# Ranks, places and scatters of a routing kernel moved by a step, and GpSimd's weight remainders cut in four

## The chip, the cores and the metric

One core of one Trainium2 chip runs the whole program. The metric is device time of one execution in microseconds, taken from several executions; the kernel before has a median of 978.65 us.

## What is computed

Three layers run one after the other on 2304 tokens (4 sequences of 576) of 512 features. The part that the change touches is the first and the routing of the second:

```
scores = scale * q @ k^T ; bias, causal mask, window of 128     (8 heads of 64)
x      = softmax(scores) @ v                                    -> 2304 x 512
logits = x @ w_gate + log1p(exp(x @ w_noise)) * noise           (8 experts)
top2   = the two largest logits of a token, softmax weights over the two
out    = sum over the two of weight * relu(x @ w1[e]) @ w2[e]   (w1 512x1024, w2 1024x512)
y      = relu(out @ w_in)^2 @ w_out                             (2048 wide, float32 in and out)
```

## The kernel before

**Stages.** For the first 140 us or so the kernel does attention and routing; then the eight experts (until some 600 us), then the last layer. The matmuls of the later stages are float32 products made of three passes: each weight is split into a rounded high part and a remainder. While attention runs, GpSimd splits the first eight weight chunks (`prep_one("pool", "pool")`, lines 97 to 112): a copy of 128x1024 into the rounded type (L108) and a subtraction of 128x1024 for the remainder (L110), two inputs from SBUF.

**The attention loop** (lines 553 to 575) has 36 working steps `v`, each for 128 query rows and 4 of the 8 heads, two steps to a block of 128 tokens. The order is written out by hand; each engine takes its instructions in that order. In step `v` come: `s_step(v+2)`, the score matmuls (L257, on some steps masked columns first, L246) into a double bank of tag "b", and on VectorE four reductions (L262: bias, and the row's extreme) that read this bank, then four exponentials on ScalarE (L268); `t_step(v+1)`, six transposes (L279) into two banks of tag "a" and their copies on ScalarE (L281); the slot 4 of the step; `pv_step(v)`, the products with v (L303) into another "b" bank; `norm` (L314, L317, L320, VectorE), which reads that bank, and every second step a store to DRAM (L326) and loads on SP's queue; `prep_one` on every fourth step; the slot 5. Tag "b" has two banks, so the scores of step `v+1` can start only when the four reductions of step `v` have read theirs. Tag "a" has three banks, tag "c" one.

**Routing** is hung into these steps by `at(step, slot, function, ...)`; slots 0 to 3 lie behind the four reductions of the step on VectorE. A pair `p` is 256 tokens, four steps. With v = 4p+3: the transposes of the block for the gate (`gate_t`, L333, bank "c") stand in slot 4 of steps 4p+3 and 4p+4, the gate's matmuls (`gate_w`, `gate_m`, L344 and L352) in 4p+5, and the selection of two experts (`gate_o`, L363 to L377, VectorE) in slots 0 to 2 of step 4p+6. Of these L363, L375 and L377 read two operands from SBUF. `rank` (lines 379 to 390: ten small matmuls, L387, into bank "c", and two additions to `acc` on VectorE, L390) stands in slot 5 of step 4p+6; `place` (lines 392 to 423: `n` = 0, L397, reads the rank's bank; the rest ends in `pos`, L422) in slots 0 to 3 of step 4p+7. The `scatter` of the pair's first block, two indirect DMAs of GpSimd (L428), stands in slot 3 of step 4p+7, that of the second in step 4p+8.

**The first expert's input.** Rows of the first three tiles are gathered before all tokens are placed: `early_table` reads the slot table back (L501, SP), `gather` fetches the rows (L441, GpSimd), `x_in` transposes them (L448, a bank "a"), copies (L449, ScalarE) and subtracts (L450, VectorE, which is the last reader of that bank). For the first two tiles they stand in steps 17, 18, 20 and 25, 26, 28.

The planner of a step, in lines 521 to 532:

```
        o = v + 2 if end else v + 3
        for n, c in enumerate((0, 0, 0, 1, 2)):
            at(o, c, gate_o, p, n)
        at(o, 4 if end else 5, rank, p)
        for n, c in enumerate((0, 1, 1, 2, 2, 3)):
            at(o + 1, c, place, p, n)
        at(o + 1, 3, scatter, 2 * p)
```

Of the kernel before, what the change touches and what calls it, by code (L numbers as in the profile page):

```python
# [11 lines left out]
F32 = mybir.dt.float32  # L12
# [5 lines left out]
OP = mybir.AluOpType  # L18
# [11 lines left out]
PARTS = (6, 10, 14)  # L30
# [19 lines left out]
def attn_moe_ffn(ctx: ExitStack, tc: tile.TileContext, qt, kt, vt, wgn, noise, w1, w2, w_in, w_out,  # L50
                 consts, out):
    nc = tc.nc
# [18 lines left out]
    def bank(tag):  # L71
        if tag == "b":
            return psum.tile([128, 2, 512], F32, name="psb", tag="b", bufs=2)
        return psum.tile([128, 512], F32, name="ps" + tag, tag=tag, bufs={"a": 3, "c": 1}[tag])
# [13 lines left out]
    def load_to(n):  # L88
        while nload[0] < min(n, len(srcs)):
            i = nload[0]  # L90
            src, a = srcs[i]
            r = rawp.tile([128, 1024], F32, name="raw", tag="raw", bufs=2)
            nc.sync.dma_start(out=r if a is None else r.rearrange("p (a d) -> p a d", a=a), in_=src)
            raws[i] = r
            nload[0] += 1

    def prep_one(hi="act", lo="dve"):
        i = nprep[0]
        nprep[0] += 1
        load_to(i + 1)  # L100
        r = raws.pop(i)
        g, m = (i // 4) % 3, (i % 4) * 2048
        t = big["wb" if g else "wa"] if g < 2 else late["wc"]
        c = [t[:, m:m + 1024], big["wt"] if g == 1 and m == 6144 else t[:, m + 1024:m + 2048]]
        if hi == "act":
            nc.scalar.activation(out=c[0], in_=r, func=AF.Copy)  # L106
        else:
            nc.gpsimd.tensor_copy(c[0], r)  # L108
        eng = nc.vector if lo == "dve" else nc.gpsimd
        eng.tensor_tensor(out=c[1], in0=r, in1=c[0].bitcast(F32), op=OP.subtract)  # L110
        chunks[i] = c
        load_to(i + 2)

# [108 lines left out]
    todo = {}  # L222

    def at(v, slot, f, *a):
        todo.setdefault((v, slot), []).append((f, a))
# [152 lines left out]

    def rank(p):
        oh = G["oh", p]  # L380
        rk = bank("c")[:, 0:16].rearrange("p (q w) -> p q w", q=2)
        G["rk", p] = rk
        for q in range(2):
            terms = [(tri, oh[:, q])] + [(ones, oh[:, 0])] * q + [(ones, acc)]
            for m, (l, r) in enumerate(terms):
                for k in range(2):
                    nc.tensor.matmul(rk[:, q, :], l, r[:, k, :], start=(m + k == 0),  # L387
                                     stop=(m + k == len(terms)))
        for q in range(2):
            nc.vector.tensor_tensor(out=acc, in0=acc, in1=oh[:, q], op=OP.add)  # L390
# [123 lines left out]
    last = NV - 1  # L514
    for p in range(NT // 2):
        v = 4 * p + 3
        end = v == last
        at(v - end, 4, gate_t, 2 * p)
        at(v + 1, 4, gate_t, 2 * p + 1)
        at(v + 2, 0 if end else 4, gate_w, p)  # L520
        at(v + 2, 0 if end else 5, gate_m, p)
        o = v + 2 if end else v + 3
        for n, c in enumerate((0, 0, 0, 1, 2)):
            at(o, c, gate_o, p, n)
        at(o, 4 if end else 5, rank, p)
        for n, c in enumerate((0, 1, 1, 2, 2, 3)):
            at(o + 1, c, place, p, n)
        at(o + 1, 3, scatter, 2 * p)
        if end or 2 * p + 2 == PARTS[-1]:
            at(o + 1, 4, scatter, 2 * p + 1)  # L530
        else:
            at(o + 2, 3, scatter, 2 * p + 1)
    at(3, 3, more_consts)
    at(4, 4, zero_rows)
    for j, (v, w, x) in enumerate(((17, 18, 20), (25, 26, 28), (2 * PARTS[-1] + 3, 2 * PARTS[-1] + 4, last + 1))):
        at(v, 4, early_table, j)
        at(w, 5, gather, 0, j, True)
        at(x, 5, x_in, 0, j)
# [14 lines left out]
    for v in range(-2, NV + 3):  # L553
        s_step(v + 2, v)
        if 0 <= v + 1 < NV:
            t_step(v + 1)
        run(v, 4)
        if 0 <= v < NV:
            i, g = divmod(v, 2)
            pv_step(v)  # L560
            for n in range(3):
                norm(i, g, n)
            if g:
                if nq < NT:
                    load_q(nq)
                    nq += 1
                while nv < 5 * B and v_free(nv - 5) <= 2 * i + 1:
                    load_v(nv)
                    nv += 1
                if nk < B and 2 * i + 1 >= 9 * (nk - 1) + 1:  # L570
                    load_k(nk)
                    nk += 1
            if v % 4 == 2 and nprep[0] < 8:
                prep_one("pool", "pool")
        run(v, 5)
# [33 lines left out]
    for c in range(16):  # L609
        c = 8 * (c % 2) + c // 2  # L610
# [85 lines left out]
    def side_work(e, f):  # L696
        if f % 2 == 1 and nprep[0] < 8 * e + 12 and (e, f) != (E - 1, 7):
            prep_one()
        if e:
            next(decode, None)  # L700
        if e and e + 1 < E and f >= 3:
            gather(e + 1, f - 3)
# [251 lines left out]
    last = E - 1  # L954
    for e in range(last):
        if e == 0:
            py = bank("c")
            for f in range(8):
                mm2(0, 0, f, py)
                if f in (4, 5):  # L960
                    x_in(0, f - 1)
                if f in (5, 7):
                    prep_one()
            y_out(0, 0, py)
            for j in range(NJ):
                gather(1, j)
# [163 lines left out]
    end = 56 * NSB  # L1130
# [85 lines left out]
    for n, (s, u, kk) in enumerate(batches):  # L1216
# [8 lines left out]
        for k in range(2):  # L1225
            st, en = kk + k == 0, kk == 3 and k == 1
            for m, (p, o, lead) in enumerate(((P1, b13[:, 0:256], True), (P2, b26[:, 0:256], True),
# [8 lines left out]
                late_ = (3 * s + u) % 2  # L1236
                if m == 0:
                    p1, u3 = tmp[2 + late_][:, 0:256], tmp[late_][:, 0:256]
                    x, y = [rows.tile([128, DM], F32, name="x", tag="r", bufs=6) for _ in range(2)]
# [71 lines left out]
```

## Time and profile before

| | |
|---|---|
| median of 3 executions | 978.65 us (977.57 to 979.04) |
| the profiled execution | 978.19 us, span 976.1 us |
| TensorE matmul busy | 957.3 us (98%) |
| VectorE busy | 674.8 us (69%) |
| ScalarE busy | 463.8 us (48%) |
| GpSimd busy | 419.2 us (43%) |

The span is what the profiler sees of the program; some 2 us of the execution lie around it. Busy time of TensorE includes the modelled ends of pipelined matmuls, so a wait shorter than such an end doesn't show as idle time; the starts of the instructions show it. In the timeline a row gives the start, the length, the engine, the line, the operation, the operands and, in brackets, the idle time before it and what ended it.

### The profile page before, as it was taken

The numbers are of one execution on the slowest core, as the hardware profiler recorded it, in microseconds if no ns is written. First come the engines' busy times: TensorE is split into PE (matmuls) and PEld (weight loads), VectorE is DVE, ScalarE is ACT, GpSimd is POOL, SyncE is SP. The second block draws the span as 40 slices with busy tenths as digits, with TensorE's granted clock in tenths as the row PEclk, the third lists the DMA queues.
The fourth block names the chain that finished last, engine by engine and source line by source line (L and its number), as shares of the span: only waits on it lengthen the run. The fifth ranks groups of instructions, "written<-read, shape, count | busy, mean of one in ns | idle before, by whom it ended". The sixth has DMA issues, their size and how long they took to land. (4 is left out here: it accounts for less than half of the span.)

```text
span 976.1 us, 19647 instructions
## 1 busy us (share of the span) xinstructions
PE 957.3 (98%) x7438; PEld 879.1 (90%) x7438; DVE 674.8 (69%) x1432; ACT 463.8 (48%) x887; POOL 419.2 (43%) x453
## 2 busy tenths in 40 slices
PE   8899999999999999999999999999999999999998
PEld 6677779898998989899898898999999998999998
DVE  5777754757686776766764436778576999877773
ACT  6677743434343343433343446655554564434331
POOL 0665543124242333425334032624221667988880
PEclk9999999999999999999999999999999999999999
DMA  8777525456667575656555453976538774444331
GB/s 277 273 237 279 198 88 152 135 166 226 197 212 241 161 234 197 219 204 207 202 190 200 148 174 94 299 203 181 151 99 240 227 213 156 145 140 129 130 108 44
DMA packets 118198, 179.99 MB, mean 184 GB/s; under 512 B 11232, under 2 KB 66288, under 8 KB 117712
## 3 DMA queue, kind: packets, MB, share of 16 engines
q1 hardware_dynamic: 107120, 146.77, 46.9%
q0 software_dynamic: 10976, 31.90, 10.6%
q8 instruction: 59, 0.97, 0.4%
q14 instruction: 43, 0.35, 0.1%
HBM read 124.33 MB, written 54.30 MB: 183 GB/s over the span
## 5 line engine op out<-in xcount | busy, mean ns | idle before, releaser
L872 POOL TENSOR_TENSOR gs<-xb 128x256 f32<-128x256 f32 x72 | 69.5, 985 | 29.3 <-DVE wc L872 13.0
L476 ACT ACTIVATE ha<-psa 128x384 fp32r<-128x384 f32 x64 | 31.3, 491 | 93.3 <-PE psa L472 91.8
L268 ACT ACTIVATE p<-p,mx 128x192 f32<-128x192 f32 x144 | 57.6, 450 | 30.3 <-DVE mx L262 29.5
L689 POOL TENSOR_TENSOR et<-ex,et 128x512 f32<-128x512 f32 x16 | 20.9, 1304 | 112.3 <-DVE ex L685 112.3
L710 POOL DMA_INDIRECT yr<-yg,pos x36 | 36.1, 1003 | 68.4 <-DVE ha L477 44.9
L477 DVE SCALAR_TENSOR_TENSOR ha<-psa,ha 128x384 fp32r<-128x384 f32 x64 | 35.4, 553 | 43.0 <-ACT ha L476 38.0
L428 POOL DMA_INDIRECT slots<-tok,pos x36 | 35.0, 972 | 46.1 <-DVE rs L314 29.6
L472 PE MATMUL psa<-xa,wa 128*128 128x384 f32 x288 | 53.4, 336 | 0.3 <-DVE ha L477 0.3
L472 PE MATMUL psa<-xa,wc 128*128 128x384 f32 x288 | 53.4, 336 | 0.0
L791 PE MATMUL psb<-wa,ha 128*128 128x512 f32 x216 | 52.8, 396 | 0.0
L441 POOL DMA_INDIRECT xr<-xd,gidx x40 | 44.3, 1108 | 19.2 <-issue 6.0
L262 DVE CUSTOM_DVE_ANT_0 p<-psb,bias 128x192 f32<-128x192 f32 x144 | 45.8, 352 | 7.7 <-PE psb L257 6.8
L472 PEld LDWEIGHTS psa<-xa,wa 128*128 128x128 f32 x288 | 49.4, 188 | 0.6 <-DVE ha L477 0.5
L472 PEld LDWEIGHTS psa<-xa,wc 128*128 128x128 f32 x288 | 49.6, 188 | 0.2
L795 ACT ACTIVATE yo<-psb 128x512 f32<-128x512 f32 x38 | 22.7, 598 | 54.3 <-PE psb L791 40.8
L872 DVE TENSOR_TENSOR wc<-gs,wc 128x512 fp32r<-128x512 f32 x48 | 48.5, 1049 | 0.0
L689 POOL TENSOR_TENSOR ex<-ex 128x512 f32<-128x512 f32 x12 | 15.6, 1303 | 74.8 <-DVE ex L685 74.8
L886 POOL DMA_DIRECT2D raw<-w x49 | 27.2, 560 | 47.0 <-DVE wb L872 18.4
L791 PEld LDWEIGHTS psb<-wa,ha 128*128 128x128 f32 x216 | 39.5, 188 | 7.8
L791 PE MATMUL psb<-wb,ha 128*128 128x512 f32 x176 | 46.3, 398 | 0.0
L110 DVE TENSOR_TENSOR wa<-raw,wa 128x1024 fp32r<-128x1024 f32 x20 | 25.3, 1266 | 30.0 <-ACT wa L106 29.9
L303 PEld LDWEIGHTS psb<-v,pt 64*64 64x64 f32 (+1 forms) x1056 | 33.1, 136 | 11.6 <-issue 7.9
(327 smaller groups left out, 2742.6 us busy)
## 6 DMA issues: line engine op xcount, KB each, us to landing
raw<-in_w_dram SPq DMA_DIRECT2D x64, 512.0 KB, 5.3
xb<-gmid SPq DMA_DIRECT2D x72, 256.0 KB, 2.7
v<-in_vt_dram SPq DMA_DIRECT2D x20, 520.0 KB, 6.7
yg<-yo SPq DMA_DIRECT2D x40, 256.0 KB, 2.5
raw<-w POOLq DMA_DIRECT2D x36, 256.0 KB, 3.9
gmid<-yo SPq DMA_DIRECT2D x48, 192.0 KB
ex<-in_w_in_dram SPq DMA_DIRECT2D x16, 512.0 KB, 4.4
ex<-in_w_out_dram SPq DMA_DIRECT2D x16, 512.0 KB, 3.4
```

Of the source, the lines that this page charges most:

```text
L262: nc.vector.tensor_tensor_reduce(out=p2[j][:, a, :], in0=ps[:, a, j, :], in1=bias[:, 4 * g + 2 * j + a, :], op0=OP.add, op1=OP.min, scale= ...
L268: nc.scalar.activation(out=p2[j][:, a, :], in_=p2[j][:, a, :], func=AF.Exp, bias=mx[j][:, a:a + 1], scale=-1.0)
L303: nc.tensor.matmul(px[64 * x:64 * x + 64, a, j, :], l, r, start=not any(m[:2] == (x, a) for m in mms[:n]), stop=not any(m[:3] == (x, a, j) ...
L428: st = nc.gpsimd.indirect_dma_start(out=slots, out_offset=bass.IndirectOffsetOnAxis(ap=pos[:, i, k:k + 1], axis=0), in_=tok[:, i:i + 1], i ...
L441: nc.gpsimd.indirect_dma_start(out=XR[e, j], out_offset=None, in_=xd[0:PARTS[j] * 128] if early else xd, in_offset=bass.IndirectOffsetOnAx ...
L472: nc.tensor.matmul(o, w[wp][:, f * 128:(f + 1) * 128], x[:, xp, d, :], start=(n == 0), stop=(n == 11))
L476: nc.scalar.activation(out=hi, in_=ps, func=AF.Relu)
L477: nc.vector.scalar_tensor_tensor(out=lo, in0=ps, scalar=0.0, in1=hi.bitcast(F32), op0=OP.max, op1=OP.subtract)
L689: nc.gpsimd.tensor_tensor(out=x, in0=af, in1=cf, op=OP.add)
L710: nc.gpsimd.indirect_dma_start(out=YR[i, k], out_offset=None, in_=yg, in_offset=bass.IndirectOffsetOnAxis(ap=pos[:, i, k:k + 1], axis=0))
L791: nc.tensor.matmul(py, h[:, hq], wc[wp][:, wsl], start=(f + n == 0), stop=(f == 7 and n == 2))
L872: f(**a)
```

## The change

`rank` of the pairs 0 to 5 goes from slot 5 of step 4p+6 to slot 4 of step 4p+7, ahead of what stands there, and uses a bank of tag "a" (for all pairs). For these pairs `place` 0 goes to slot 5 of step 4p+7 and the other places to slots 0 to 2 of step 4p+8; the scatters go to steps 4p+8 and 4p+9. The pairs 6 to 8 keep their order. For the first two tiles the table, the gather and `x_in` stand in steps 18, 19, 22 and 26, 27, 30. GpSimd subtracts a weight remainder in four pieces of 128x256.

```diff
@@ -106,8 +106,10 @@
-        eng = nc.vector if lo == "dve" else nc.gpsimd
-        eng.tensor_tensor(out=c[1], in0=r, in1=c[0].bitcast(F32), op=OP.subtract)
+        eng, step = (nc.vector, 1024) if lo == "dve" else (nc.gpsimd, 256)
+        for n in range(0, 1024, step):
+            sl = slice(n, n + step)
+            eng.tensor_tensor(out=c[1][:, sl], in0=r[:, sl], in1=c[0][:, sl].bitcast(F32), op=OP.subtract)
@@ -378,7 +380,7 @@
-        rk = bank("c")[:, 0:16].rearrange("p (q w) -> p q w", q=2)
+        rk = bank("a")[:, 0:16].rearrange("p (q w) -> p q w", q=2)
@@ -522,17 +524,24 @@
-        at(o, 4 if end else 5, rank, p)
-        for n, c in enumerate((0, 1, 1, 2, 2, 3)):
-            at(o + 1, c, place, p, n)
-        at(o + 1, 3, scatter, 2 * p)
+        late_ = 2 * p + 2 < PARTS[-1]
+        q = o + 2 if late_ else o + 1
+        if late_:
+            todo.setdefault((o + 1, 4), []).insert(0, (rank, (p,)))
+            at(o + 1, 5, place, p, 0)
+        else:
+            at(o, 4 if end else 5, rank, p)
+            at(q, 0, place, p, 0)
+        for n, c in enumerate((0, 1, 1, 2, 2) if late_ else (1, 1, 2, 2, 3)):
+            at(q, c, place, p, n + 1)
+        at(q, 3, scatter, 2 * p)
         if end or 2 * p + 2 == PARTS[-1]:
-            at(o + 1, 4, scatter, 2 * p + 1)
+            at(q, 4, scatter, 2 * p + 1)
         else:
-            at(o + 2, 3, scatter, 2 * p + 1)
+            at(q + 1, 3, scatter, 2 * p + 1)
-    for j, (v, w, x) in enumerate(((17, 18, 20), (25, 26, 28), (2 * PARTS[-1] + 3, 2 * PARTS[-1] + 4, last + 1))):
+    for j, (v, w, x) in enumerate(((18, 19, 22), (26, 27, 30), (2 * PARTS[-1] + 3, 2 * PARTS[-1] + 4, last + 1))):
```

## Rows read from the trace of the kernel before

**Rows 1.** Busy time by stretch: time, length, PE, PEld, DVE, ACT, POOL, PEclk, DMA, GB/s.

```profile
50.00:100.00 50.00, 48.45 (x885) 36.69 (x882) 37.53 (x236) 39.92 (x104) 29.62 (x40) 1.00 0.74 253
...
150.00:200.00 50.00, 50.00 (x294) 44.40 (x293) 26.24 (x44) 19.05 (x30) 10.60 (x10) 1.00 0.53 164
```

**Rows 2.** Waits of PE, whole span: us in total, times, longest.

```profile
PE psc L387 <- DVE oh L375: 1.7, 5, 0.6
```

**Rows 3.** Timeline of step 14 (pair 2, the step 4p+6), PE and DVE.

```profile
58.33 0.88 PE L257 MATMUL psb<-k,q 64*64 64x192 f32 x16
...
59.39 0.36 DVE L262 CUSTOM_DVE_ANT_0 p<-psb,bias 128x192 f32<-128x192 f32 x1 [0.61 <-PE psb L257]
...
59.95 1.13 PE L303 MATMUL psb<-v,pt 128*64 128x65 f32 x32
...
61.14 0.18 DVE L375 TENSOR_TENSOR oh<-iota,sel 128x32 bf16<-128x32 uint32 x1
61.25 0.15 DVE L377 TENSOR_TENSOR gap<-gs 128x2 f32<-128x2 f32 x1
...
61.39 0.20 PE L387 MATMUL psc<-oh,tri 128*128 128x8 bf16 x2 [0.31 <-DVE oh L375]
...
61.59 0.08 DVE L262 DVE_READ_ACCUMULATOR2_ANT mx<- 128x1 f32 x1
...
61.82 0.88 PE L257 MATMUL psb<-k,q 64*64 64x192 f32 x16
```

**Rows 4.** Timeline of step 15 (pair 2, the step 4p+7), PE, DVE and POOL.

```profile
62.76 0.36 DVE L262 CUSTOM_DVE_ANT_0 p<-psb,bias 128x192 f32<-128x192 f32 x1
...
63.92 1.13 PE L303 MATMUL psb<-v,pt 128*64 128x65 f32 x32
...
64.94 0.08 DVE L262 DVE_READ_ACCUMULATOR2_ANT mx<- 128x1 f32 x1
64.94 0.16 DVE L422 TENSOR_TENSOR pos<-gs,cst 128x4 int32<-128x4 f32 x1
...
65.07 0.30 PE L246 MATMUL psb<-far,ones 64*64 64x256 bf16 x4
...
65.37 0.99 POOL L428 DMA_INDIRECT slots<-tok,pos  x1 [5.44 <-DVE rs L314]
```

**Rows 5.** Timeline of step 6 (pair 0, the step 4p+6), DVE and PE.

```profile
30.94 2.31 DVE L377 TENSOR_TENSOR gap<-gs 128x2 f32<-128x2 f32 x1
...
33.58 0.30 PE L246 MATMUL psb<-far,ones 64*64 64x256 bf16 x2 [2.09 <-DVE mx L262]
```

**Rows 6.** Busy time and clock in step 7, columns as in rows 1.

```profile
34.50:37.00 2.50, 2.50 (x14) 2.15 (x14) 2.27 (x18) 1.58 (x5) 0.00 (x0) 0.50 0.92 371
```

**Rows 7.** Timeline around step 18 (pair 3): GpSimd's chunk and VectorE's L363.

```profile
70.19 1.06 POOL L108 CAST wb<-raw 128x1024 fp32r<-128x1024 f32 x1
...
71.33 2.35 POOL L110 TENSOR_TENSOR wb<-raw,wb 128x1024 fp32r<-128x1024 f32 x1
...
73.26 0.45 DVE L363 TENSOR_TENSOR gs<-gs,nz_sb 128x16 f32<-128x16 f32 x1
```

**Rows 8.** GpSimd's subtractions of line 653: ns minimum/median/maximum, first and last start.

```profile
L653 POOL TENSOR_TENSOR tt<-et,tt x16: 722/741/815, 372.9 to 526.9; 128x256 f32<-128x256 f32 x16
```

**Rows 9.** Timeline, end of step 12 and start of step 13, PE.

```profile
53.64 1.13 PE L303 MATMUL psb<-v,pt 128*64 128x65 f32 x32
...
54.59 0.83 PE L257 MATMUL psb<-k,q 64*64 64x192 f32 x16
```

**Rows 10.** Timeline: `x_in` behind step 20; copies of the transposes of step 30.

```profile
82.24 0.66 PE L448 MATMUL psa<-cst,xr 128*128 128x128 f32 x4
...
83.67 0.69 DVE L450 TENSOR_TENSOR xa<-psa,xa 128x512 fp32r<-128x512 f32 x1 [0.46 <-ACT xa L449]
...
118.12 0.85 ACT L281 ACTIVATE pt<-psa 128x384 f32<-128x384 f32 x2
```

**Rows 11.** Waits of SP's queue, 0 to 160 us: us in total, times, longest.

```profile
SPq L501 <- DMA slots<-tok,pos: 19.4, 3, 11.5
```

## The prediction

> **What bounds the kernel now.** I read the busy time by stretch first. In the experts' stretch TensorE is busy all of the time, in attention 48.45 of 50 us, at the full clock [rows 1]. So what attention gains or loses in TensorE's order of work reaches the end: behind it no idle time stands that could take it up or give it back. The waits of TensorE come next: the rank's matmuls wait for VectorE's one-hot five times, 1.7 us in all [rows 2]. This is the wait that the new order removes, and the most that this list promises.
>
> Then I read the timeline of one pair, since a busy share doesn't tell which wait ends last. In step 14 (4p+6) the scores start at 58.33, the first reduction at 59.39, L375 at 61.14, L377 at 61.25, the rank's matmuls at 61.39; the last reduction's readout ends at 61.59 + 0.08 = 61.67 and the next scores start at 61.82 [rows 3]. So when the rank has run, the bank of the scores has just come free: both wait for the same VectorE work. The six pairs from 1 to 6 all show the next scores within 0.15 us of the last readout. In step 15 (4p+7), with `place` between the reductions, the readout ends at 64.94 + 0.08 = 65.02 and the next scores start at 65.07 [rows 4]: VectorE again, by a little. A pair has one or two steps bound by the chain scores, reductions, bank, scores; the others are TensorE's.
>
> **The parts.** The profiled execution took 978.19 us, 0.46 under the median of the three; the sum is made against it.
>
> (a) Four pieces, pair 0. L377, 0.15 us elsewhere [rows 3], takes 2.31 us in step 6, and the next scores follow it after a wait of 2.09 [rows 5]. It reads two operands from SBUF; GpSimd began a subtraction just ahead of it, and L377 ends with it. [...] The same is seen smaller at pair 3: L363 starts inside a subtraction of 2.35 us that begins at 71.33 and, at 73.26 + 0.45 = 73.71, ends 0.03 behind it [rows 7]. A piece of 128x256 takes 0.74 us [rows 8], so L377 waits for at most one: 2.31 - 0.74 = 1.57, of which I take 1.5. With some 1.2 us of idle time left instead of 2.1 and more, I take the clock to stay up: 1.2 more. Sum -2.7 (bounds 0, were a second piece and the slow clock to follow, and -3.4, were L377 to wait for none). For GpSimd itself 4 x 0.74 - 2.35 = 0.6 us more a chunk, eight times; nothing waits for the chunks before the experts, so I cost this at nothing. Without that cover it would be 4.9.
>
> (b) Rank out of step 4p+6. The next scores still wait for the last readout. By step 15 they can follow it by 0.05 instead of 0.15 [rows 3, 4]: six times 0.07, -0.4 (bounds 0, and the -1.7 of the wait list).
>
> (c) Rank into step 4p+7. `place` is gone from the reductions there, so TensorE's own work sets the step. Scores can follow the products by 0.95 (53.64 to 54.59) [rows 9], here they take 65.07 - 63.92 = 1.15 [rows 4], so 0.20 is free. The rank takes 61.82 - 61.39 = 0.43 of TensorE's order [rows 3], some 0.3 of it issue. So +0.1 a pair, +0.6 (bounds -1.2 and +2.6). The two additions to `acc` move with it, behind the reductions, where VectorE has time.
>
> (d) `place` into step 4p+8. The chain from the first reduction to the last readout stays, 65.02 - 62.76 = 2.26 [rows 4]: of its small operations L397 leaves it and L422 comes in. But `norm` and L397 now stand ahead of the first reduction of a step that follows a full TensorE step, so I put this reduction 1.1 behind the scores, not the 0.94 of step 15 (62.76 - 61.82) [rows 3, 4]. With 0.1 to the next scores that is 3.5 us, against 3.25 for the place step before (65.07 - 61.82) and about that for the 4p+8 steps: +0.2 for five pairs, and some 0.6 for pair 0, whose step 8 is short of work: +1.6 (bounds 0 and +3). The scatters go with it, behind each other on GpSimd in the same order. SP waits for their landing ahead of the table read, 19.4 us in three waits [rows 11]; read and scatter move together, and the stores and loads behind the read have a step's time, so I cost this at nothing. Without that cover a late load of q would stop TensorE for a microsecond or so.
>
> (e) `x_in` two steps later. Its transposes leave steps 20 and 28, 0.66 us each [rows 10], some 0.6 of it issue; I take -1.25 for both. They go to steps 22 and 30, whose TensorE idles for the chain, so their own time is free. Their banks are not. The last reader is L450 on VectorE, 0.69 us, behind a copy on ScalarE [rows 10], which stands behind the copies of the transposes; those run late in a 4p+6 step, from 118.12 for 0.85 us in step 30 [rows 10], when the next scores have started. Behind step 22 the rank of pair 4 needs that very "a" bank, three allocations on, and would wait about 1.0. In step 30 the rank of pair 6 stands ahead of `x_in` and takes a bank, so the transposes wait for the first copy of 118.12 and push the first reduction of the following place step by 1.8. Sum -1.25 + 1.0 + 1.8 = +1.55 (bounds -1.25 and +3).
>
> (f) The collision. GpSimd's chunk follows the four scatters of a pair without a pause: L422 at 64.94 [rows 4], copy at 70.19, subtraction at 71.33 [rows 7], 6.39 behind L422. L422 moves into the next step and one reduction forward, to 2.9 behind its scores. So the pieces run from 2.9 + 6.4 = 9.3 to 12.3 behind the scores of step 4p+8. The selection of the next pair is two steps on, 3.5 + 3.7 = 7.2 (the second from 54.59 to 58.33 [rows 9, 3]), with L375 2.81 and L377 2.92 behind its scores [rows 3]: 10.0 and 10.1. Before, the subtraction ended just ahead of or within L363; now L375 and L377 fall into its pieces. The first goes at the end of the running piece, almost at once; the second then faces a whole one, 0.74 [rows 8]. The last reduction stands behind L377, and the next scores behind that: six pairs (1 to 6) times 0.74 = +4.4 (bounds 0, and two waits and a blocked L363, 1.6 a pair, +9.6). I take one piece, as both instructions are nearest to the case of L377 in rows 5. In exchange the tails of the long subtraction on L363 go (0.45 at pair 3 instead of 0.17, smaller twice): -0.5.
>
> Sum: -2.7 - 0.4 + 0.6 + 1.6 + 1.55 + 4.4 - 0.5 = +4.55. Against the profiled execution that is 982.7, against the median 983.2: **983.0 us**.
>
> **Rivals.** *The copy blocks too.* L363 stands 1.34 behind its scores, 8.5 on the scale of (f), inside GpSimd's copy (8.2 to 9.3). No row of before shows an instruction with two SBUF inputs beside a copy. Were it held as by a subtraction, L363 would wait 0.75 and L375 and L377 0.85 more: (f) is 6 x 1.6 = 9.6, the time 978.2 + 0.15 + 9.6 = 988.0. [...]
>
> [...]
>
> [...]
>
> *The clock falls each time.* The steps 4p+6 then idle TensorE by 0.6 + 0.74 and more; were 1.25 lost behind each as in rows 6, 983.0 + 7.5 = 990.5. Against it: it was seen only behind 2.1.
>
> **How the numbers follow.** Forecast 0.50, copy 0.13, miss 0.20, miss with free banks 0.12, clock 0.05. The range from 976.5 to 988.0 holds the first three with the bounds of the small terms (about 1.8 below the miss, and the copy's sum above) and leaves out the last two, 0.17. A measurement of this kernel can tell 0.2%, 1.96 us. Faster: the 0.12 and 0.04 of the miss, 0.16; same: 0.14 of the miss and 0.03 of the forecast, 0.17; slower: 0.67.
>
> **What would show it.** Right: L377 of step 6 near 0.8 instead of 2.31 and no clock of 0.50 behind it; the scores behind steps 10, 14, ... still within 0.1 of the last readout; L375 or L377 of these steps at 0.5 us and more beside GpSimd's pieces; the rank of pair 4 waiting for L450. Wrong: L375 and L377 at their 0.15 to 0.2 in most pairs, steps 4p+6 shorter than 3.3, or a 4p+7 step that grows by the whole rank.

## The result, and the profile after

The changed kernel takes **993.22 us** (median of 6 runs, 986.88 to 995.26) against 978.71 for the kernel before in the same session (6 runs): a ratio of 1.014, 95% interval 1.0118 to 1.0163. It is slower, as forecast, but by 14.5 us where the forecast of 983.0 had some 4, and outside the range of 976.5 to 988.0. Its profiled execution took 989.1 us (span 987.0, mean granted clock 0.995).

Busy time by stretch, columns as in rows 1:

```profile
50.00:100.00 50.00, 42.90 (x770) 33.38 (x768) 37.06 (x220) 34.52 (x88) 25.09 (x40) 0.97 0.66 221
100.00:150.00 50.00, 43.57 (x698) 34.14 (x699) 33.42 (x194) 30.04 (x77) 26.47 (x44) 0.93 0.42 130
```

In attention TensorE was busy 48.45 of 50 us [rows 1]; now it is 42.90, and its granted clock is no longer full (PEclk 0.97 and 0.93). The waits of PE over the whole span (us in total, times, longest) say for whom:

```profile
PE psb L259 <- DVE rs L316: 7.9, 7, 1.9
PE psb L248 <- DVE mx L264: 4.3, 5, 1.7
PE psa L450 <- ACT pt L283: 1.4, 1, 1.4
...
PE psa L389 <- DVE oh L377: 0.7, 1, 0.7
PE psa L389 <- DVE xa L452: 0.7, 1, 0.7
```

The rank's wait of rows 2 has fallen from 1.7 to 0.7, with another 0.7 for a bank of `x_in`. In its place the scores (L248, L259: L246 and L257 of before) wait for VectorE twelve times, 1.0 us on average; before, the list had one such wait, the 2.09 of rows 5. Three instructions of VectorE make it late. By line: ns minimum/median/maximum, first and last start (L365, L377 and L379 are L363, L375 and L377 of before):

```profile
L365 DVE TENSOR_TENSOR gs<-gs,nz_sb x9: 174/599/748, 27.7 to 147.5; 128x16 f32<-128x16 f32 x9
...
L377 DVE TENSOR_TENSOR oh<-iota,sel x9: 191/294/307, 29.3 to 148.6; 128x32 bf16<-128x32 uint32 x9
...
L379 DVE TENSOR_TENSOR gap<-gs x9: 155/728/732, 29.5 to 148.7; 128x2 f32<-128x2 f32 x9
```

The timeline of step 14 (the step of rows 3) shows how:

```profile
57.14 1.05 POOL L108 CAST wa<-raw 128x1024 fp32r<-128x1024 f32 x1
...
57.66 0.58 DVE L365 TENSOR_TENSOR gs<-gs,nz_sb 128x16 f32<-128x16 f32 x1
...
58.28 2.77 POOL L112 TENSOR_TENSOR wa<-raw,wa 128x256 fp32r<-128x256 f32 x4
...
59.44 0.29 DVE L377 TENSOR_TENSOR oh<-iota,sel 128x32 bf16<-128x32 uint32 x1
...
59.66 0.73 DVE L379 TENSOR_TENSOR gap<-gs 128x2 f32<-128x2 f32 x1
...
60.59 0.08 DVE L264 DVE_READ_ACCUMULATOR2_ANT mx<- 128x1 f32 x1
...
60.81 0.88 PE L259 MATMUL psb<-k,q 64*64 64x192 f32 x16 [1.75 <-DVE rs L316]
```

L365 ends at 58.24, 0.05 behind the end of GpSimd's copy at 58.19. The remainder's four pieces (2.77 in all, 0.69 each) start at 58.28 and end at about 58.97, 59.67, 60.36 and 61.05. L377 starts late in the second and ends at 59.73, L379 ends at 60.39: each just behind the end of a piece, L379 after a whole one. The last reduction stands behind both, and the scores behind its readout. The holds are 0.41 + 0.10 + 0.58 = 1.09 us a pair (0.58, 0.29 and 0.73 less the 0.17, 0.19 and 0.15 of undisturbed ones).

Step 6 (pair 0) went as (a) had it: L379 is held 0.73 instead of 2.31 [rows 5], and no half clock follows in this execution (PEclk 1.00 from 30.57 to 38.00):

```profile
29.51 0.73 DVE L379 TENSOR_TENSOR gap<-gs 128x2 f32<-128x2 f32 x1
...
30.57 0.30 PE L248 MATMUL psb<-far,ones 64*64 64x256 bf16 x2 [1.51 <-DVE mx L264]
```

The half clock (PEclk 0.50; the 16 score matmuls behind step 18 take 1.56 us instead of 0.88) has moved to two other pairs, behind step 18 and from step 30 on, 3 and 6 us long. At half the work in that time they would cost 1.5 and 3.0 us; this is an estimate from these lengths, and an upper one where TensorE also waits:

```profile
76.00:79.00 3.00, 3.00 (x29) 2.31 (x30) 1.71 (x10) 2.09 (x6) 0.18 (x1) 0.50 1.00 392
124.00:130.00 6.00, 5.69 (x45) 4.34 (x46) 3.31 (x21) 3.23 (x8) 0.40 (x1) 0.50 0.01 1
```

The banks show in step 23, where the rank of pair 4 waits for the addition of `x_in` (L452, once L450), and in step 30, where the transposes of `x_in` wait for ScalarE's copy:

```profile
94.17 0.69 DVE L452 TENSOR_TENSOR xa<-psa,xa 128x512 fp32r<-128x512 f32 x1 [1.02 <-ACT xa L451]
...
94.91 0.19 PE L389 MATMUL psa<-oh,tri 128*128 128x8 bf16 x2 [0.66 <-DVE xa L452]
...
124.31 1.12 PE L450 MATMUL psa<-cst,xr 128*128 128x128 f32 x4 [1.40 <-ACT pt L283]
```

Measured from the first scores of a step to those of the next, and summed by kind over steps 8 to 32, the profiled executions give (the last column is of e10 below, the changed kernel with GpSimd's chunk elsewhere):

| steps | before | after | e10 |
|---|---|---|---|
| 4p+6 (10, 14 ... 30) | 20.61 | 28.96 | 21.77 |
| 4p+7 (11 ... 31) | 19.69 | 23.65 | 20.74 |
| 4p+8 (8 ... 32) | 23.65 | 24.01 | 24.29 |
| 4p+9 (9 ... 29) | 22.34 | 23.13 | 23.09 |
| sum | 86.29 | 99.75 | 89.89 |

So 13.46 us are lost in these steps, 8.35 of them in the steps of the selection. Steps 6 and 7 gain 2.65 (10.18 to 7.53), and the experts start 9.2 later (146.83 for 137.62).

The spread of the runs goes with the clock. Of the six runs the shortest, 986.88, had a mean granted clock of 0.998, the longest, 995.26, one of 0.990: 0.008 less over 990 us is 7.9 us of work at the full clock by estimate, about the whole difference of 8.4.

### The profile page after: what moved, and what is told of

Its sections match the earlier page's. It is cut to its first block, busy times and chain, and to the rows that moved or that the text cites. A ratio compares the mean times of both kernels' runs of the same rounds, so it can differ in the third digit from the quotient of the medians.

```text
span 987.0 us, 19672 instructions
## 1 busy us (share of the span) xinstructions
PE 957.2 (97%) x7438; PEld 880.3 (89%) x7438; DVE 680.4 (69%) x1432; ACT 463.9 (47%) x887; POOL 423.7 (43%) x477
```

## The experiments

Ten runs in three sessions. The kernel before had medians of 978.63, 978.75 and 979.2 in them, and each ratio is to its own session. "The chunk" is GpSimd's copy and remainder of one weight block.

**e1: the kernel before with the four pieces alone.**

```diff
-        eng = nc.vector if lo == "dve" else nc.gpsimd
-        eng.tensor_tensor(out=c[1], in0=r, in1=c[0].bitcast(F32), op=OP.subtract)
+        eng, step = (nc.vector, 1024) if lo == "dve" else (nc.gpsimd, 256)
+        for n in range(0, 1024, step):
+            sl = slice(n, n + step)
+            eng.tensor_tensor(out=c[1][:, sl], in0=r[:, sl], in1=c[0][:, sl].bitcast(F32), op=OP.subtract)
```

> The kernel before with nothing but the four pieces of GpSimd's remainder. My theory (the pieces bound the wait of the one instruction of pair 0, and with it the clock stays up): the last selection instruction of step 6 takes 0.7 us instead of 2.31, no stretch at half clock behind it, 1.5 + 1.2 = 2.7 us less, so about 976.0 us. Rival (pieces are themselves the harm, as four pieces last 2.77 us where one lasts 2.35): the first product of the selection (L363 of before) is held in more pairs, the time stays at 978 to 980.

Measured: 978.29 (12 runs), ratio 1.0001, 0.9987 to 1.0015. In its profile the long wait of pair 0 is gone: the difference is held 0.73 at most,

```profile
L365 DVE TENSOR_TENSOR gs<-gs,nz_sb x9: 171/189/749, 27.6 to 134.8; 128x16 f32<-128x16 f32 x9
...
L379 DVE TENSOR_TENSOR gap<-gs x9: 154/155/733, 29.3 to 136.0; 128x2 f32<-128x2 f32 x9
```

steps 6 and 7 take 7.43 instead of 10.18, and the experts start at 134.17, 3.45 earlier. The span is only 0.7 shorter: from the last layer's first matmul to its last it took 368.5 us, against 366.1 in the profiled execution of before. The rival came in two pairs: the product was held by a piece in steps 14 and 26 (0.68 and 0.75 us), which grew by 0.42 and 0.44. So the 2.75 of steps 6 and 7 are in the profile and not in the median, which was expected at 976.0; by the interval the gain is at most some 1.3 us. e8 bears on the reason.

**e2: the changed kernel with the remainder in one operation again.**

```diff
-        eng, step = (nc.vector, 1024) if lo == "dve" else (nc.gpsimd, 256)
-        for n in range(0, 1024, step):
...
+        eng = nc.vector if lo == "dve" else nc.gpsimd
+        eng.tensor_tensor(out=c[1], in0=r, in1=c[0].bitcast(F32), op=OP.subtract)
```

> The changed kernel with the remainder in one operation again. My theory (the place of GpSimd's chunk beside the selection costs, and pieces soften it): the difference instruction (L379 of the changed kernel) waits for the whole 2.35 us subtraction, some 1.3 to 1.9 us instead of 0.73 in six pairs, 4 to 7 us more and more stretches at half clock: 997 to 1003 us. Rival (the pieces are the harm, each gives VectorE another turn to lose): 985 to 990 us, faster than the changed kernel.

Measured: 997.78 (4 runs), ratio 1.021, 1.0185 to 1.0234. With a single long operation it is the one-hot that is held, in most pairs, and not the difference, as expected; the difference behind it runs free:

```profile
L375 DVE TENSOR_TENSOR oh<-iota,sel x9: 193/1230/1244, 30.7 to 154.1; 128x32 bf16<-128x32 uint32 x9
...
L377 DVE TENSOR_TENSOR gap<-gs x9: 147/148/155, 31.8 to 154.3; 128x2 f32<-128x2 f32 x9
```

Four stretches of 3 us at 0.50 follow, behind steps 10, 14 and 18 and from step 30 on; the first of them:

```profile
49.00:52.00 3.00, 3.00 (x34) 2.61 (x33) 1.31 (x10) 2.72 (x7) 0.00 (x0) 0.50 0.66 266
```

In the new order the pieces are therefore worth some 4.6 us; in the old one (e1) nothing that can be told.

**e3: the changed kernel, the difference moved out of the selection** into a part of `place`, two steps on, where no chunk runs.

```diff
-            nc.vector.tensor_tensor(out=gap[:, two, None], in0=gs[:, 3, :, 1:2], in1=gs[:, 3, :, 0:1], op=OP.subtract)
...
         if n == 1:
+            two = slice(2 * p, 2 * p + 2)
+            nc.vector.tensor_tensor(out=gap[:, two, None], in0=gs[:, 3, :, 1:2], in1=gs[:, 3, :, 0:1], op=OP.subtract)
```

> The changed kernel with the difference of the two largest logits (two operands from SBUF, needed only behind attention) taken out of the selection and put into the place step. My theory: its 0.73 us, of which 0.58 is waiting, leave the chain of six pairs, 0.6 to 0.7 a pair, 4 us, and TensorE idles 1.2 instead of 1.9 us there, so that the clock holds: under 986 us, the granted clock near 0.998. Rival (another chain, the bank of the rank or of the x transposes, sets the steps): the time stays at 990 us or above.

Measured: 985.13 (4 runs), ratio 1.0064, 1.0042 to 1.0086. The place of one small instruction accounts for 8.1 of the 14.5 us. Held time explains 6 x 0.58 = 3.5 of it; the rest goes with the clock, whose mean is 0.997 to 1.0 in these runs and 0.989 to 0.998 in those of the changed kernel. This split is an estimate. What stays is the product, held beside the copy (median length 0.58):

```profile
L365 DVE TENSOR_TENSOR gs<-gs,nz_sb x9: 171/580/744, 28.7 to 141.1; 128x16 f32<-128x16 f32 x9
...
L403 DVE TENSOR_TENSOR gap<-gs x9: 152/155/158, 35.2 to 145.0; 128x2 f32<-128x2 f32 x9
```

**e4: the changed kernel, with the chunk made to start behind the selection.** A copy of one element of the difference on GpSimd, ahead of the chunk, from the second chunk on.

```diff
             if v % 4 == 2 and nprep[0] < 8:
+                if v > 2:
+                    nc.gpsimd.tensor_copy(spacer, gap[0:1, (v - 6) // 2:(v - 6) // 2 + 1])
                 prep_one("pool", "pool")
```

> The changed kernel with one small GpSimd copy that reads the difference of the pair ahead of each chunk from the second on, so that GpSimd's copy and pieces start behind the selection instead of beside it. My theory: the three held instructions return to 0.17, 0.19 and 0.15 us, some 1.1 us a pair off the chain and no half clock there; about 986.9 (the fastest execution of the changed kernel, whose clock fell least) minus 6.6 to 7, so 980 us, and what is left over 978.65 is the move of rank, places and x. Rival (the move of the rank into TensorE's order and the banks is the cost): 986 us or above though the three instructions are short.

Measured: 981.38 (12 runs), ratio 1.0034, 1.0018 to 1.0049. Nothing else is changed, and 11.8 of the 14.5 us are gone, 0.9 of them in steps 6 and 7 (6.60 instead of 7.53 in the profiles). Timeline of step 14:

```profile
57.31 0.19 DVE L377 TENSOR_TENSOR oh<-iota,sel 128x32 bf16<-128x32 uint32 x1
57.41 0.15 DVE L379 TENSOR_TENSOR gap<-gs 128x2 f32<-128x2 f32 x1
...
57.70 0.18 POOL L584 COPY spacer<-gap 1x1 f32<-1x1 f32 x1 [2.30 <-DVE gap L379]
57.83 1.03 POOL L108 CAST wa<-raw 128x1024 fp32r<-128x1024 f32 x1
57.99 0.88 PE L259 MATMUL psb<-k,q 64*64 64x192 f32 x16 [0.65 <-DVE rs L316]
...
58.94 2.79 POOL L112 TENSOR_TENSOR wa<-raw,wa 128x256 fp32r<-128x256 f32 x4
...
60.05 1.02 DVE L392 TENSOR_TENSOR acc<-acc,oh 128x16 bf16<-128x16 bf16 x2
```

The selection runs at its undisturbed times and the next scores wait 0.65. That wait is no loss: in this place the rank's matmuls stood before [rows 3], and the step takes 3.40 where it took 3.49. GpSimd now holds the additions to `acc` (1.02 for two, 0.36 in step 6 of the kernel before), behind the last reduction, and nothing waits for them. Five of the six steps 4p+6 take 3.29 to 3.40, the level of before. So the collision with the chunk is shown as the cause of most of the loss. The half clock behind step 18 is gone with it (the 16 score matmuls take 0.88 us there); the mean granted clock is 0.997 in this execution, and 1.0 in that of e10, the same kernel.

**e5: e4 with `x_in` a step earlier**, in steps 21 and 29.

```diff
-    for j, (v, w, x) in enumerate(((18, 19, 22), (26, 27, 30), (2 * PARTS[-1] + 3, 2 * PARTS[-1] + 4, last + 1))):
+    for j, (v, w, x) in enumerate(((18, 19, 21), (26, 27, 29), (2 * PARTS[-1] + 3, 2 * PARTS[-1] + 4, last + 1))):
```

> The kernel of the fourth experiment (chunks behind the selection) with the transposes of the first two tiles one step earlier, in steps 21 and 29 instead of 22 and 30. My theory: the rank of pair 4 no longer waits for a bank that VectorE still reads, and the transposes of step 29 find theirs; steps 23, 30 and 31 lose 0.85, 1.4 and 0.7 us, steps 21 and 29 gain 0.6 each by TensorE's own work: 1.8 us less than the fourth experiment's 981.4, so 979.6, within 0.2% of the kernel before; that is then what the move of the rank by itself is worth: nothing. Rival (the move of ranks and places costs by itself): 981 or above.

Measured: 984.16 (6 runs), ratio 1.0052, 1.0031 to 1.0072: not the 979.6 that was expected, and by the medians worse than e4, though the intervals overlap. The profiled execution is the slowest of the six (987.93). In it the rows that `x_in` transposes land too late for step 21:

```profile
80.93 0.99 POOL L443 DMA_INDIRECT xr<-xd,gidx  x1 [2.78 <-PE psb L305]
...
88.09 1.11 PE L450 MATMUL psa<-cst,xr 128*128 128x128 f32 x4 [3.01 <-DMA xr<-xd,gidx]
```

TensorE waits 3.0 us for the rows, and ran at 0.50 from 88 to 94 behind it. In step 29 no such wait shows (the only other one for these rows is 0.2). So with the scatters a step later, the first `x_in` can't go back that far without waiting.

**e6: the changed kernel with the copy in four pieces too.**

```diff
-            nc.gpsimd.tensor_copy(c[0], r)
+            for n in range(0, 1024, 256):
+                nc.gpsimd.tensor_copy(c[0][:, n:n + 256], r[:, n:n + 256])
```

> The changed kernel with GpSimd's copy of 128x1024 in four pieces of 128x256 too. My theory (a copy of one operand holds a VectorE instruction with two SBUF operands as a subtraction does): the first product of the selection (L365 of the changed kernel) takes at most 0.35 us instead of 0.6 in pairs 1 to 6, some 0.3 a pair, about 991 us with the clock still falling in places. Rival (the product is held by something else, the subtraction's start or ScalarE): it stays at 0.6 us, 993 us.

Measured: 989.72 (4 runs), ratio 1.011, 1.008 to 1.014. The median length of the product falls with that of the copy's operations, from 0.60 to 0.31:

```profile
L366 DVE TENSOR_TENSOR gs<-gs,nz_sb x9: 170/308/3611, 27.9 to 147.5; 128x16 f32<-128x16 f32 x9
```

That speaks for the copy as the holder. It also has a maximum of 3.61. In step 6 the product did not get in between the pieces at all:

```profile
27.31 1.42 POOL L109 CAST wa<-raw 128x256 fp32r<-128x256 f32 x4
27.89 3.61 DVE L366 TENSOR_TENSOR gs<-gs,nz_sb 128x16 f32<-128x16 f32 x1
28.70 2.76 POOL L113 TENSOR_TENSOR wa<-raw,wa 128x256 fp32r<-128x256 f32 x4
```

It started at 27.89, waited through all the pieces of copy and remainder that were left (to 31.46), and ended at 31.50. Steps 6 and 7 took 12.14 us instead of 7.53, in part at half clock, so this execution doesn't show the gain of the other pairs in full. Here the boundaries between the pieces were no opening.

**e7: the kernel before, with only the chunk moved behind the selection** (the edit of e4; ranks, places and `x_in` as before, one long remainder).

> The kernel before, its order of ranks, places and scatters untouched, with nothing but the small GpSimd copy that puts each chunk from the second on behind the selection of the pair. In this order the place instructions with two SBUF operands follow in the next step. My theory (what counts is what VectorE does beside GpSimd's chunk, not where the rank stands): the one subtraction of 2.35 us then holds the place step by some 1.5 us in seven pairs, 10 us and half clock in places: 987 to 996 us, as slow as the change. Rival (the move of the ranks makes the loss): within 1 us of 978.6.

Measured: 990.26 (4 runs), ratio 1.0104, 1.0077 to 1.0131. The same edit that helps the new order by 11.8 us hurts the old one by 11.5. In step 15 the chunk now lies on `place`:

```profile
60.16 0.15 DVE L377 TENSOR_TENSOR gap<-gs 128x2 f32<-128x2 f32 x1
...
61.69 2.37 POOL L110 TENSOR_TENSOR wa<-raw,wa 128x1024 fp32r<-128x1024 f32 x1
...
62.38 1.71 DVE L401 TENSOR_SCALAR ri<-ri 128x16 int32<-128x16 int32 x1
...
65.59 0.30 PE L246 MATMUL psb<-far,ones 64*64 64x256 bf16 x4 [1.56 <-DVE mx L262]
```

L401, 0.17 us elsewhere, is held until 64.09, the end of the subtraction (64.06), though it reads one operand only; so it is in all seven pairs that have a chunk beside them (1.71 each). Steps 4p+7 take 4.85 to 5.04 instead of 3.25 to 3.30. This is a loss of the same size without any rank moved, by the place of the chunk alone.

**e8: the kernel before, unchanged**, a second execution of pair 0.

> The kernel before once more, for a second profile. My theory (the 2.31 us wait and the half clock of pair 0 hang on when a load of 512 KB lands, and so on the execution): the last selection instruction of step 6 is another length than 2.31, or the stretch behind it is at full clock, and the time is still within 976 to 981.5. Rival (the wait is there in every execution): 2.2 to 2.35 us and 0.50 again; then the gain that the four pieces show there is lost later.

Measured: one run of 981.34. The remainder began earlier against the selection, it was the product that ran into it, and the difference was free:

```profile
29.12 2.36 POOL L110 TENSOR_TENSOR wa<-raw,wa 128x1024 fp32r<-128x1024 f32 x1
...
30.43 1.09 DVE L363 TENSOR_TENSOR gs<-gs,nz_sb 128x16 f32<-128x16 f32 x1
```

Steps 6 and 7 take 4.23 and 3.26, with no half clock (the transposes of step 7 take 0.88, 1.54 in the execution of rows 6): what e1 reached with pieces. So the 2.31 of rows 5 and the clock of rows 6 belong to one of two executions, and not to the kernel as such; how often they come isn't known.

**e9: e4 with `x_in` in steps 24 and 32**, away from the ranks (the edit of e5 with other numbers), and **e10: e4 again** beside it.

> The changed kernel with GpSimd's chunk behind the selection (the experiment that came to 981.4, 2.75 over before), and x_in in steps 24 and 32, where no rank stands ahead of it or close behind it, instead of 22 and 30. If the rest of the loss is the "a" bank that x_in and the ranks of pairs 4 and 6 pass to each other: the waits of the transposes on pt (1.4) and of the rank on xa (0.7) are gone, step 23 falls from 4.1 to about 3.4 and steps 30 and 31 together from 8.7 to about 7, and the time is 979.0 (978 to 980). If the rest is the place steps 4p+8 and other things, steps 23 and 30 to 31 stay in sum what they were or x_in's cost only goes to steps 24 and 32, and the time stays at 981.4 (980.5 to 982.5).

> The same kernel as the one with the chunk behind the selection, for comparison on the same chip: 981.4 (980.5 to 982.5) by either theory.

Measured: 980.83 (12 runs), ratio 1.0024, 1.0006 to 1.0042; and 981.0 (11 runs), ratio 1.0023, 1.0005 to 1.004. In e9 the waits on `x_in`'s banks are gone; in e10 they are there,

```profile
PE psa L450 <- ACT pt L283: 0.8, 1, 0.8
PE psa L389 <- DVE xa L452: 0.6, 1, 0.6
```

yet the time is the same. Steps 22, 23 and 30 fall from 3.51, 4.02 and 4.76 to 3.40, 3.29 and 3.40, but steps 25, 31 and 32 rise from 3.90, 3.97 and 3.22 to 4.68, 4.64 and 3.92; over steps 8 to 32 it is 89.98 against 89.89. So the first of the two theories falls: the banks delay those steps, but without them as much is lost elsewhere. What remains of e4, some 2 us over before, is not traced further than the last column of the table.

No version that was run beats the kernel before; e1 equals it.

## Why the prediction failed in size

- **(f), the collision: right in kind and place, too small.** Counted from the scores of step 12 (48.93), the copy ran from 8.21 to 9.26 (8.2 to 9.3 by the prediction's scale), L365 began at 8.73 (8.5), the pieces ran from 9.35 to 12.12 (9.3 to 12.3) and L377 began at 10.51 (10.0). The step that failed is the price, "I take one piece, as both instructions are nearest to the case of L377 in rows 5": 4.4 less 0.5. The second instruction does wait for one piece (0.73), as forecast, but L365 is held by the copy as well, 0.41, and L377 for 0.10. That is the rival *the copy blocks too*, given 0.13, and L365 at 0.58 agrees with it. Its 1.6 a pair was too high: holds of 1.09 match steps 10 to 26, which grew by 1.06 on average (22.63 against 17.31 for five); six pairs make 6.4. With the clock that went with them, the chunk's place was worth 11.8 us (e4). What the chances call a miss is (f) at nothing (978.3, or 975.5 with (e) at -1.25). Its 0.32 was an estimate, and with L379 at 0.73 in all seven pairs that have a chunk beside them it did not come.
- **The clock: put at nothing, by the wrong argument.** I gave the rival 0.05 because the 0.50 of rows 6 was seen only behind a wait of 2.1. Here it came behind 1.84 (step 18). In the profiled execution it cost 4.5 by the estimate above, which is too much: holds of 6.4 leave 3.5 of the 9.86 by which the table's last two columns differ. I also put the copy and the clock down as alternatives, though longer holds make the idle times longer: the range ended at the copy's sum alone, 988.0. With their measured sizes, (a) at nothing, (b) to (e) at 3.60 and the holds at 6.4 make 10.0 of the 14.5 us. The 4.5 that are left (the same figure only by chance) are put down to the clock; that is an estimate, as no run changes the clock alone.
- **(a), pair 0: right in the profile, nothing in the median.** Between the two profiled executions steps 6 and 7 gained 2.65, as forecast 2.7. But e8 has the kernel before without that stall, and e1 the same median as before. I took a wait that occurs once in a profile for a property of the kernel. The sum without (a) would have been 985.7. No run shows the 1.2 that (a) puts on the clock by itself: in e1, with the transposes of step 7 at 0.88 instead of 1.54, steps 6 and 7 took 2.75 less. The wait ahead of the scores fell by 1.57 of that (2.09 to 0.52), and 1.18 is left for the clock, an estimate by difference. The claim that attention's gain reaches the end holds for the experts (467 to 469 us from their first matmul to the last layer's first in before, after, e1, e8 and e10). The last layer's matmuls took 366.1 us in the profile of before and 368.1 to 368.9 in the other four, up to 2.8 more, which hid e1's gain between the two profiles.
- **(b) and (c), the rank: about right.** Steps 11, 15 and 27, without half clock or `x_in`, take 9.62 together instead of 9.85. The rank costs nothing there. The way of (b) didn't show: in step 14 the scores follow the readout by 60.81 - 60.67 = 0.14, as before, and not by 0.05. (Its 0.07 a pair was also less than the 0.10 between its two rows.)
- **(d), the place: about right, in part at another spot.** Steps 8, 12, 16, 24 and 32 grew by 0.86 (16.69 against 15.83; 1.14 in e10), and steps 4p+9, which the forecast left out, by 0.79. 1.6 was forecast.
- **(e), `x_in`: waits right, gain too large.** The rank of pair 4 lengthens step 23 by 0.88 (1.0 forecast). Steps 30 and 31 are 2.14 longer even without the collision (e10; 1.8 forecast). But leaving steps 20 and 28 gained 0.5 together, not 1.25, as I read it because a place came in there. All of (b) to (e) is 3.60 by the table, against 3.35 forecast. That the sum comes so close is in part luck: by the steps of e10, (b) and (c) came to -0.7 (0.2 forecast), (d) to 1.9 (1.6) and (e) to 2.4 (1.55). The one term that depends on two engines meeting missed by more.

Of the signs that were to show it right, L379 of step 6 at 0.73, no 0.50 behind it, L379 held beside the pieces and the rank of pair 4 waiting for `x_in` came; the scores behind step 14 followed the readout by 0.14, not within 0.1.

## What to carry to other kernels

Before moving small VectorE operations, lay GpSimd's SBUF work over the new order and ask which of them end only with a running GpSimd operation; price each by that operation's length (in e7 it was 1.71 beside one of 2.37), plain copies included (in step 14 0.58 beside one of 1.05), and add the clock that the longer idle times may cost (0.50 for 3 us behind step 18). When two rivals share a cause, add them: they come together. A stall seen once in a profile is priced only when a second execution shows it.

## What the runs showed of the hardware

- In the changed kernel a plain copy on GpSimd held VectorE's product, as the subtraction's pieces held L379 (0.73): L365, 0.17 undisturbed, took 0.41 to 0.75 beside the copy of 1.05 and ended 0.05 behind it in step 14, and 0.04 to 0.05 behind it in all seven pairs that have a chunk beside them.
- Not only operations on two SBUF operands were held: L401, one int32 operand with a constant, took 1.71 instead of 0.17 (e7). Its hold ended 0.03 behind the end of a subtraction of 2.37. Beside the chunk of step 14 the maxima (L370, 0.24 for two) and the index searches (L373, 0.16) kept the times that they have in step 6 of the kernel before (0.24 and 0.16).
- Pieces didn't always give an opening: in e6 one product waited 3.61 through all the pieces that were left, where the median was 0.31.
- Half clock did not follow each long wait of TensorE. In the changed kernel it came behind 1.84 (step 18), not behind 1.92 (step 10) or 1.75 (steps 14 and 26); in e2 behind 2.28, 2.11 and 2.20 (steps 10, 14, 18), not behind 2.10 (step 26); in e7 behind 1.56 in step 15 (0.50 from 68 to 70), not behind 1.56, 1.62 and 1.71 in steps 7, 11 and 19, where the 24 to 32 products next behind the wait took 1.06 to 1.13 and not 1.83. What decides between them the runs don't show.
